# Masking the scores on GpSimd for two heads at once, and zero products in the values' PSUM banks

## The chip, the cores and the metric

The kernel runs on one NeuronCore of a Trainium2 chip. The metric is the device time of one execution in microseconds (us). Engines are named as the profile names them: PE is TensorE (its weight loads are PEld), DVE is VectorE, ACT is ScalarE, POOL is GpSimd, and SP is the engine that issues the DMAs.

## The reference: what is computed

Causal attention with a forgetting bias for 8 batches of 8 heads (576 positions, 64 columns a head, float32), and then a feed-forward block with a convolution of three taps and a gate.

```python
scores = scale * np.matmul(q, k.transpose(0, 1, 3, 2))
causal = np.triu(np.ones((S, S), dtype=bool), k=1)
cum = np.cumsum(np.maximum(s, 0.0), axis=-1)
bias = -(cum[:, :, :, None] - cum[:, :, None, :])
scores = np.where(causal, -1000000000.0, scores + np.minimum(bias, 0.0))
attn = np.exp(scores - np.max(scores, axis=-1, keepdims=True))
attn = attn / (np.sum(attn, axis=-1, keepdims=True) + 1e-09)
x = np.matmul(attn, v)                    # heads side by side: 8 x 576 x 512
...
h = np.maximum(x @ w_in, 0.0)             # 512 -> 1024
conv_out[t] = sum(conv_w[k] * h[t + k - 1] for k in range(3))
out = (h * (1.0 / (1.0 + np.exp(-conv_out)))) @ w_out      # 1024 -> 512
```

## The kernel before

**Work and its order.** Heads are worked on in 32 pairs: the two heads of a pair lie in the lower and the upper 64 partitions, and a product of 64 rows belongs to one of them. Four pairs make a batch, and when a batch's four pairs are done its feed-forward block follows. All work is written as tasks (`add(name, [(engine, planned duration)], dependencies, tag, ...)`). A list scheduler (`Sched.play`) then lays the tasks out once, when the program is built: at each moment it gives every engine the ready task with the smallest tag, where the planned durations say when an engine is free again. The tags come from the table `DUE`, one number for each task. What comes out is a fixed order of instructions for each engine. On the chip each engine works through its order strictly, and an instruction that waits holds up all that stand behind it.

**A pair.** The tasks of pair p, and the lines of the kernel before:

- The loads: `raw` (q and k), `bb` (the bias, spread over 128 partitions), `v`, `ek` (bias rows).
- `hi` and `lo` (L1032, L1036) split q and k into a rounded part and a rest. `lo` runs on POOL or DVE and takes all of `raw`.
- `sh0` to `sh3` (L1102): a first set of score products, in four parts with two PSUM banks each, of which only the row maxima are wanted. The causal mask is added by a product of a mask with a unit matrix (L1109) for the first seven pairs, and by a cut of `bb` on POOL (L1075) from then on. DVE takes the maxima (L1135).
- `turn` (L1161) transposes the maxima on PE. ACT copies them (L1169), and a DMA puts them into `eq`.
- `sc0` to `sc3` (L1209): the score products proper, four for each piece, the last of which (`eq`, `ek`) adds bias and maximum. For the first eight pairs (`p < B0`) a mask product on PE (L1213) stands in each of the five pieces with a diagonal, one for each head. For the other 24 pairs POOL zeroes the part above the diagonal after the exponential, ten `affine_select` a pair (L1244).
- The exponentials (L1231, ACT) go to the tiles `pt`, one for each head.
- From pair 7 on (`dense`) the exponentials of the key tiles 1 to 3 are added up, head by head, on DVE or POOL (L1292). `sum` (L1328, PE) makes the row sums, `pv` (L1269, PE) the product with the values into the two PSUM banks `pv`.
- The normalisation: ACT copies the sums (`gd`, L1344), DMAs gather them (`rc`), DVE takes the reciprocal (L1355), DMAs write it out and spread it (`ri_d`, `rb`), DVE multiplies (`nm`, L1378), ACT or DVE rounds (`xh`, L1393), DVE or POOL takes the rest (`xl`, L1397). `pv` of the next pair waits for `nm`.

The feed-forward products are L1428 (first) and L1517 (second); ACT, DVE and POOL do ReLU, taps, gate and splitting between them. From pair 8 on the products of a pair's attention stand together as one burst.

**Zero products.** Until the planned time `AWAKE` = 112 us the scheduler puts a product of zeros (L1564, `still`, 256 columns, result unused) into every planned gap of PE, one for each 0.12 us. It needs a free score bank (`ps`, six of them): with all six taken, PE gets none. If the last product worked on one head (mode "r"), the zero product has 64 rows; otherwise 128.

Of the kernel before, what the change touches and what calls it, by code (L numbers as in the profile page):

```python
# [65 lines left out]
B0 = 8  # L66
# [492 lines left out]
def kernel(  # L559
# [133 lines left out]
    def c_tt(n):  # L693
        return 0.155 + n / 0.96e3
# [134 lines left out]
    def rest(e):  # L829
        nc.vector.scalar_tensor_tensor(  # L830
            s_sb, cum, 8.0 * EK, grid, op0=ALU.subtract, op1=ALU.subtract
        )

    t_rest = add("rest", [("DVE", 1.5, True)], [t_cum], -140, rest)

    def bias_mm(e):
        for t in range(NT):
# [795 lines left out]
```

## Time and profile before

| what | value |
| --- | --- |
| time, median of 3 runs | 771.92 us (771.81 to 774.02) |
| profiled execution, its own time | 774.2 us |
| its span, first to last instruction | 772.5 us |
| PE busy / weight loads | 752.9 us (97%) / 669.8 us (87%) |
| DVE, ACT, POOL busy | 490.7 us (64%), 464.5 us (60%), 387.3 us (50%) |
| mean granted TensorE clock | 0.985 |
| zero products (L1564) | 149 |
| mask products in the scores (L1213) | 80 |
| `affine_select` on the exponentials (L1244) | 240 |
| additions of the exponentials (L1292) | 86 on DVE, 64 on POOL |

Read the table with the granted clock in mind: a busy PE counts zero products, mask products and slow products alike. All times below are from the span's start.

### The profile page before, as it was taken

How to read it: one execution, taken by the hardware profiler on the slowest of the kernel's cores; microseconds unless marked ns; L12 is line 12 of the kernel's file. 1: busy time of each engine (PE TensorE's matmuls, PEld its weight loads, DVE VectorE, ACT ScalarE, POOL GpSimd, SP SyncE). 2: the span in 40 equal slices, each digit the busy share in tenths (PEclk: the TensorE clock that was granted, in tenths of full speed). 3: DMA queues.
4: the chain of work that ended last, by engine and by line, in shares of the span. 5: the costliest groups of instructions: out<-in, count | busy, mean ns of one | idle time of the engine just before them, and what ended most of it. 6: DMA issues, size and time to landing. Idle time of an engine off the chain costs nothing.

```text
span 772.5 us, 20600 instructions
## 1 busy us (share of the span) xinstructions
PE 752.9 (97%) x7856; PEld 669.8 (87%) x7856; DVE 490.7 (64%) x1414; ACT 464.5 (60%) x1084; POOL 387.3 (50%) x575
## 2 busy tenths in 40 slices
PE   5999999999999999999999999999999999999998
PEld 4676678898888989898999989999999989999998
DVE  7478888456775756767564756756686756733622
ACT  5177678456566657657565757657565656644633
POOL 6032235355636566664735666646756565532211
PEclk8599999999999999999999999999999999999999
DMA  6857762332404242241423342232423230111000
GB/s 191 257 150 242 213 205 67 113 104 84 143 27 122 87 131 95 75 143 61 131 62 114 96 131 89 85 110 76 144 65 116 93 100 25 42 33 48 17 31 31
DMA packets 55160, 80.18 MB, mean 104 GB/s; under 512 B 14041, under 2 KB 34841, under 8 KB 55001
## 3 DMA queue, kind: packets, MB, share of 16 engines
q1 hardware_dynamic: 55061, 78.87, 33.1%
q8 instruction: 61, 1.00, 0.5%
q14 instruction: 38, 0.31, 0.1%
HBM read 67.48 MB, written 10.98 MB: 102 GB/s over the span
## 4 chain that ended last, share of the span: by engine, by line
PE 83%; DVE 6%; DMA 5%; issue 3%; ACT 1%; POOL 1%; SPq 0%; DVEq 0%; POOLq 0%; ACTq 0%
PE ps L1428 26%; PE ps L1517 26%; PE ps L1209 12%; PE pv L1269 10%; PE ps L1102 4%; DMA rb<-ri_d 3%; PE ps L1328 3%; DMA ri_d<-ri 2%; DVE ps L1135 2%; PE ps L1564 1%; DMA bb<-cum_d 1%; DVE r L1135 1%; PE ps L1213 1%; DVE w L909 0%; PE ps L1161 0%
## 5 line engine op out<-in xcount | busy, mean ns | idle before, releaser
L1428 PE MATMUL ps<-x,wi 128*128 128x290 f32 x1536 | 216.9, 298 | 1.6 <-DVE ct L1477 1.5
L1517 PE MATMUL ps<-u,wo 128*128 128x288 f32 x1536 | 217.0, 297 | 0.7 <-ACT ob L1534 0.5
L1428 PEld LDWEIGHTS ps<-x,wi 128*128 128x128 f32 x1536 | 209.1, 190 | 3.4 <-DVE ct L1477 1.8
L1517 PEld LDWEIGHTS ps<-u,wo 128*128 128x128 f32 x1536 | 206.5, 189 | 3.5 <-ACT ob L1534 0.7
L1231 ACT ACTIVATE pt<-ps,bias_sb 128x288 f32<-128x288 f32 (+4 forms) x384 | 153.6, 479 | 85.2 <-PE ps L1209 85.1
L1135 DVE CUSTOM_DVE_ANT_0 ps<-ps,bb 128x64 f32<-128x64 f32 (+4 forms) x320 | 132.2, 453 | 89.4 <-PE ps L1102 44.6
L1489 POOL TENSOR_TENSOR u<-ct,u 128x576 fp32r<-128x576 f32 x64 | 91.7, 1432 | 176.5 <-ACT u L1485 126.5
L1459 DVE SCALAR_TENSOR_TENSOR ct<-ps,cw_sb,ct 128x288 f32<-128x288 f32 (+1 forms) x256 | 130.8, 514 | 62.3 <-ACT ct L1446 59.4
L1209 PE MATMUL ps<-s 64*128 64x288 f32 (+4 forms) x1152 | 121.3, 305 | 4.7 <-DVE r L1135 3.5
L1209 PEld LDWEIGHTS ps<-s 64*128 64x128 f32 x1152 | 97.7, 186 | 15.3 <-DVE r L1135 9.4
L1036 POOL TENSOR_TENSOR s<-raw,s 128x1152 fp32r<-128x1152 f32 x31 | 83.7, 2698 | 51.8 <-DVE s L1032 30.2
L1269 PE MATMUL pv<-pt,v 128*32 128x448 f32 (+4 forms) x1536 | 94.7, 389 | 1.0 <-DVE rb L1378 0.9
L1075 POOL TENSOR_SCALAR_AFFINE_SELECT bb<-bb 128x256 f32<-128x256 f32 (+1 forms) x125 | 51.5, 421 | 79.7 <-DVE r L1135 41.5
L1441 ACT ACTIVATE ps<-ps 128x289 f32<-128x289 f32 x128 | 50.9, 397 | 62.5 <-PE ps L1428 61.4
L1269 PEld LDWEIGHTS pv<-pt,v 128*32 128x32 f32 x1536 | 59.4, 110 | 31.7 <-issue 24.5
L1244 POOL TENSOR_SCALAR_AFFINE_SELECT pt<-pt 128x128 f32<-128x128 f32 (+1 forms) x240 | 71.4, 321 | 13.8 <-ACT pt L1231 13.0
L1477 DVE TENSOR_TENSOR ct<-ct,ps 128x288 f32<-128x288 f32 x128 | 57.5, 449 | 29.9 <-ACT ct L1471 29.4
L1471 ACT ACTIVATE ct<-ct 128x288 f32<-128x288 f32 x128 | 56.3, 440 | 29.7 <-DVE ct L1459 29.2
L1209 PE MATMUL ps<-eq,ek 64*128 64x288 f32 (+4 forms) x384 | 69.1, 317 | 0.0
L1446 ACT ACTIVATE ct<-ps,cw_sb 128x288 f32<-128x288 f32 x128 | 63.6, 497 | 4.6
L1102 PE MATMUL ps<-s 64*128 64x288 f32 (+4 forms) x384 | 62.7, 347 | 0.0
L1135 DVE CUSTOM_DVE_ANT_0 ps<-ps,bb,r 128x288 f32<-128x288 f32 x64 | 30.9, 523 | 40.5 <-PE ps L1102 40.3
(89 smaller groups left out, 747.3 us busy)
## 6 DMA issues: line engine op xcount, KB each, us to landing
raw<-qk SPq DMA_DIRECT2D x32, 576.0 KB
bb<-cum_d SPq DMA_DIRECT2D x32, 576.0 KB
v<-vp SPq DMA_DIRECT2D x32, 320.0 KB
rb<-ri_d SPq DMA_DIRECT2D x64, 144.0 KB
outT<-ob SPq DMA_DIRECT2D x64, 144.0 KB
w<-w_in SPq DMA_DIRECT2D x8, 512.0 KB
w<-w_out SPq DMA_DIRECT2D x8, 512.0 KB
rows_d<-bx SPq DMA_DIRECT2D x1, 1215.0 KB
```

The source lines that it names most:

```text
L1036: tt_on(e)(st[:, 0:2, :], R_t[raw.slot], st[:, 2:4, :].bitcast(F32), op=ALU.subtract)
L1102: nc.tensor.matmul(dst[j], l, S_t[sb.slot][r, 2, c0:c1], start=True, stop=not (early and diagonal(tau, c1)),)
L1135: nc.vector.tensor_tensor_reduce(out=src, in0=src, in1=in1, scale=1.0, scalar=acc if c0 else -3.0e38, op0=ALU.add, op1=ALU.max, accum_out=acc,
L1209: nc.tensor.matmul(dst[j], l, m, start=(k == 0), stop=(k == 3))
L1231: nc.scalar.activation(PT_t[pts[j].slot][0:jt, O_T[t] + c0 : O_T[t] + c1], bank(pb, o, o + c1 - c0)[0:jt], AF.Sigmoid, bias=bias_sb[0:jt, ...
L1244: nc.gpsimd.affine_select(out=reg, in_=reg, pattern=[[1, dg]], compare_op=ALU.is_ge, fill=0.0, base=0, channel_multiplier=-1,)
L1269: nc.tensor.matmul(pvt[gs, o0 : o0 + c1 - c0], vt[0:jt, t, gs], PT_t[pts[g // 2].slot][0:jt, O_T[t] + c0 : O_T[t] + c1], start=(t == 0), s ...
L1428: nc.tensor.matmul(bank(hb, 0, XW), l, r, start=(k == 0), stop=(k == len(seq) - 1))
L1446: nc.scalar.activation(C_t[ct.slot][:, i, :], bank(hb, 2 * hf, 2 * hf + HS), AF.Copy, scale=cw_sb[:, 3 * f + 1 : 3 * f + 2],)
L1459: nc.vector.scalar_tensor_tensor(cc[:, lo:hi], bank(hb, hf + sh + lo, hf + sh + hi), cw_sb[:, 3 * f + k : 3 * f + k + 1], cc[:, lo:hi], op ...
L1489: tt_on(e)(uu[:, 1], C_t[ct.slot], uu[:, 0].bitcast(F32), op=ALU.subtract)
L1517: nc.tensor.matmul(bank(pb, 0, HS), l, r, start=(fp == 0 and k == 0), stop=(fp == NF // 2 - 1 and k == len(seq) - 1),)
```

## The change

1. **Zero products.** With no score bank free, a planned gap of PE now gets a zero product that writes to the values' banks `pv`, if these are free.
2. **Masks.** The mask products L1213 are gone. All 32 pairs are masked on POOL after the exponentials, and one `affine_select` does a piece for both heads: five a pair, twice as wide. It waits for the exponentials of both heads.
3. **Sums.** One addition does a key tile for both heads: three a pair from pair 7 on in the place of six, twice as wide. For that the tiles `pt` and `ht` become slices of one tile each.
4. **Plan.** Planned durations are changed (`SH_D`, `SC_D`, masks, sums and others), and the table `DUE` has new numbers, so the order on every engine is another one.

The table is shown by two lines, from its beginning.

```diff
-    -4342, -2961, -2916, -3027, -3033, -2954, -3077, -2973, -2965, -2830, -4716, -3541, -3351,
+    -4437, -31564, -3194, -3762, -3297, -3396, -3426, -2970, -2895, -2949, -3684, -32749, -26067,
...
-                    if now < idle[0] and free and now >= awake:
-                        slot = min(free, key=lambda i: idle[5].given[i])
+                    if now < idle[0] and (free or idle[6].free) and now >= awake:
+                        slot = min(free, key=lambda i: idle[5].given[i]) if free else -1
                         t = Task()
                         if mode != "r":
                             mode = None
                         t.name, t.mode, t.then = "idle", mode, []
                         lane = [0]
-                        lanes[slot].append(lane)
+                        if free:
+                            lanes[slot].append(lane)
                         t.emit = lambda e, slot=slot, mode=mode, lane=lane: idle[4](
...
-    PT_t = [const.tile([P, O_T[-1] + W_T[-1]], F32, name=f"pt{i}") for i in range(NPT)]
+    PT_a = const.tile([P, NPT, O_T[-1] + W_T[-1]], F32, name="pt")
+    PT_t = [PT_a[:, i, :] for i in range(NPT)]
...
-    H_t = [const.tile([P, 2, XW], F32, name=f"ht{i}") for i in range(NHT)]
+    H_a = const.tile([P, NHT, 2 * XW], F32, name="ht")
+    H_t = [H_a[:, i, :].rearrange("p (a c) -> p a c", a=2) for i in range(NHT)]
...
+    SH_D = 0.2, 0.2, 0.32, 0.33
+    SC_D = 0.54, 0.63, 1.18, 1.02
...
+        def both(r0, r1, c0, c1):
+            i0, i1 = (b.slot for b in pts)
+            return PT_a[r0:r1, i0 : i1 + 1 : i1 - i0, c0:c1]
...
-                        if k == 2 and c0 == 0 and p < B0:
-                            dg = min(P, cn)
-                            for j in range(2):
-                                nc.tensor.matmul(
-                                    dst[j][:, 0:dg], mask[:, MW - P : MW], unit[:, 0:dg],
-                                    start=False, stop=False,
-                                )
...
-            t_sc = add(f"sc{p}.{i}", [("PE", 4 * sum(c_rt(c1 - c0) for _, c0, c1 in part) + (0 if p >= B0 else 0.4))], [t_ident, t_shift, t_lo], A + 0.1 * i,
+            t_sc = add(f"sc{p}.{i}", [("PE", SC_D[i])], [t_ident, t_shift, t_lo], A + 0.1 * i,
...
-                    def sc_mask(e, j=j, t=t):
-                        jt, dg = J_T[t], min(P, W_T[t])
-                        reg = PT_t[pts[j].slot][0:jt, O_T[t] : O_T[t] + dg]
-                        nc.gpsimd.affine_select(
-                            out=reg, in_=reg, pattern=[[1, dg]], compare_op=ALU.is_ge, fill=0.0,
-                            base=0, channel_multiplier=-1,
-                        )
-
-                    if c0 == 0 and p >= B0:
-                        t_exp = add(f"mk{p}.{j}.{t}", [("POOL", 0.29, True)], [t_exp],
-                                    A + 0.1 * i, sc_mask, uses=[pts[j]])
                     masks.append((t, j, t_exp))
                     o += w
+            for t, c0, c1 in part:
+                if c0:
+                    continue
+
+                def sc_mask(e, t=t):
+                    reg = both(0, J_T[t], O_T[t], O_T[t] + min(P, W_T[t]))
+                    nc.gpsimd.affine_select(
+                        out=reg, in_=reg, pattern=[[0, 2], [1, min(P, W_T[t])]],
+                        compare_op=ALU.is_ge, fill=0.0, base=0, channel_multiplier=-1,
+                    )
+
+                done = [k for k, m in enumerate(masks) if m[0] == t]
+                t_mk = add(f"mk{p}.{t}", [("POOL", 0.42 if W_T[t] >= P else 0.3, True)],
+                           [masks[k][2] for k in done], A + 0.1 * i, sc_mask, uses=pts)
+                for k in done:
+                    masks[k] = (t, masks[k][1], t_mk)
...
-        def key_sum(j, t):
+        def key_sum(t):
             def run(e):
-                a = partial(j)
-                src = PT_t[pts[j].slot]
+                i0, i1 = (b.slot for b in acc)
+                a = H_a[:, i0 : i1 + 1 : i1 - i0, 0 : S - P]
                 o = P * (t - 1)
                 (nc.vector if e == "DVE" else nc.gpsimd).tensor_tensor(
-                    a[:, o:], src[:, P : S] if t == 1 else a[:, o:],
-                    src[:, O_T[t] : O_T[t] + W_T[t]], op=ALU.add,
+                    a[:, :, o:], both(0, P, P, S) if t == 1 else a[:, :, o:],
+                    both(0, P, O_T[t], O_T[t] + W_T[t]), op=ALU.add,
                 )
             return run
...
-                for j in range(2):
-                    t_ad = add(
-                        f"ad{p}.{j}.{t}",
-                        [("DVE", c_tt(W_T[t]), True), ("POOL", c_pool(W_T[t]), True, 2.0)],
-                        [m for k, h, m in masks if h == j and (k == t or t == 1 and k == 0)]
-                        + ([added[-2]] if t > 1 else []),
-                        tq - 4, key_sum(j, t), alloc=[acc[j]] if t == 1 else [],
-                        uses=[pts[j]] + ([acc[j]] if t > 1 else []),
-                    )
-                    added.append(t_ad)
+                t_ad = add(
+                    f"ad{p}.{t}",
+                    [("DVE", c_tt(2 * W_T[t]) + 0.07, True), ("POOL", c_pool(2 * W_T[t]), True, 2.0)],
+                    [m for k, h, m in masks if k == t or t == 1 and k == 0] + added[-1:],
+                    tq - 4, key_sum(t), alloc=acc if t == 1 else [],
+                    uses=pts + (acc if t > 1 else []),
+                )
+                added.append(t_ad)
...
-            ps_t[slot][:, 0:AWAKE_N], still[r, 0:P], still[r], start=True, stop=True
+            (pvt if slot < 0 else ps_t[slot])[:, 0:AWAKE_N], still[r, 0:P], still[r], start=True, stop=True
...
-        (AWAKE, t_still, 0.005 + AWAKE_N * 0.42e-3, AWAKE_T, stay_awake, pool_ps)
+        (AWAKE, t_still, 0.005 + AWAKE_N * 0.42e-3, AWAKE_T, stay_awake, pool_ps, pools["pv"])
```

Three places show how the order moves. The first is PE, after the maxima products of pair 0 have filled all six score banks (`ps_65` to `ps_70`); what follows are five transposes of the bias table (L838 before, L830 now) that need a bank given back. Before:

```order
L1102 MATMUL ps_69<-s_83 128x64
L1102 MATMUL ps_70<-s_83 128x64
L1109 LDWEIGHTS unit
L1109 MATMUL ps_69<-mask,unit 128x64
L1109 LDWEIGHTS unit
L1109 MATMUL ps_70<-mask,unit 128x64
L838 MATMUL ps_65<-ident,pt_97 128x64 x4
L838 MATMUL ps_65<-ident,pt_97 64x64
```

Now, the first two rows of the zero products that stand in between:

```order
L1104 LDWEIGHTS unit
L1104 MATMUL ps_69<-mask,unit 128x64
L1104 LDWEIGHTS unit
L1104 MATMUL ps_70<-mask,unit 128x64
L1559 LDWEIGHTS still
L1559 MATMUL pv<-still 128x256
```

and the last ones:

```order
L1559 LDWEIGHTS still
L1559 MATMUL pv<-still 128x256
L1559 LDWEIGHTS still
L1559 MATMUL pv<-still 128x256
L830 MATMUL ps_65<-ident,pt 128x64 x4
L830 MATMUL ps_65<-ident,pt 64x64
```

In all 56 zero products, which write to `pv`, now stand ahead of the transposes; they have 64 rows. Further on, 45 zero products stood between the transposes and pair 0's first score product; now there are 33. In the whole program there are 241 in the place of 149, all ahead of the first feed-forward product in both.

The second place is ACT, when pair 1's sums are ready and pair 0's normalised values are to be rounded. Before (`x<-rb` is pair 0's rounding, `rs<-ps` pair 1's copy of the sums, `rt` the next pair's maxima):

```order
L894 ACTIVATE w_5121_302<-w_10240_301 128x512
L899 ACTIVATE w_5122_303<-w_10240_301,tail_sb 128x512
L1393 CAST x<-rb 128x2x290
L1344 ACTIVATE rs<-ps_69 128x144
L894 ACTIVATE w_5121_308<-w_10240_307 128x512
L899 ACTIVATE w_5122_309<-w_10240_307,tail_sb 128x512
L1169 ACTIVATE rt_103<-ps_65,base_sb 10x64 x2
```

Now:

```order
L886 ACTIVATE w_5121_358<-w_10240_357 128x512
L891 ACTIVATE w_5122_359<-w_10240_357,tail_sb 128x512
L938 CAST wi<-w_5122_356 128x4x128
L1339 ACTIVATE rs<-ps_66 128x144
L1388 CAST x<-rb 128x2x290
L1163 ACTIVATE rt_101<-ps_65,base_sb 10x64 x2
```

The copy of the sums now stands ahead of the rounding, which waits for the normalisation of the pair before; it is so for the next pairs too.

The third place is POOL, after the last of its preparations (`v`), during the first pairs. Before:

```order
L717 AFFINE_SELECT v_95<-v_95 64x640
L1036 TENSOR_TENSOR s_83<-raw_81,s_83 128x1152
L949 TENSOR_TENSOR wi<-w_5122_306,wi 128x4x128
L1036 TENSOR_TENSOR s_84<-raw_82,s_84 128x1152
L1397 TENSOR_TENSOR x<-rb,x 128x2x290
```

Now:

```order
L709 AFFINE_SELECT v_95<-v_95 64x640
L1241 AFFINE_SELECT pt<-pt 128x2x128
L1241 AFFINE_SELECT pt<-pt 64x2x64
L1241 AFFINE_SELECT pt<-pt 128x2x128
L1031 TENSOR_TENSOR s_83<-raw_82,s_83 128x1152
L1241 AFFINE_SELECT pt<-pt 128x2x128 x2
L941 TENSOR_TENSOR wi<-w_5122_353,wi 128x4x128
L1241 AFFINE_SELECT pt<-pt 128x2x128 x2
L1031 TENSOR_TENSOR s_84<-raw_81,s_84 128x1152
```

The masks of the pairs' scores (`pt<-pt`) are new here, and the splitting of a later pair's q and k (`s<-raw,s`) stands between the masks of one pair.

## Rows read from the trace of the kernel before

**Rows 1.** Windows: us, busy per engine (instructions), granted clock, DMA share, GB/s

```profile
12.00:17.20 5.20, 0.00 (x0) 0.00 (x0) 2.48 (x7) 4.06 (x7) 3.79 (x5) 0.51 0.96 258
17.20:35.50 18.30, 18.27 (x90) 11.36 (x90) 10.25 (x47) 2.07 (x7) 0.00 (x0) 0.50 0.87 268
...
40.00:109.30 69.30, 67.39 (x935) 46.28 (x931) 56.24 (x161) 51.42 (x111) 19.70 (x11) 1.00 0.71 214
109.30:769.30 660.00, 654.03 (x6741) 602.63 (x6732) 411.29 (x1185) 398.08 (x946) 354.40 (x535) 1.00 0.28 85
```

**Rows 2.** PE, 0 to 50 us: start, length, line, operation, rows x columns, count

```profile
1.72 7.03 PE L1564 MATMUL ps<-still 128*128 128x256 bf16 x47 [1.72 <-DVE still L755]
...
17.23 0.80 PE L838 MATMUL ps<-ident,pt 64*128 64x64 f32 x5 [6.78 <-DVE r L1135]
...
27.42 4.87 PE L1564 MATMUL ps<-still 64*128 64x256 bf16 x22
...
34.34 1.09 PE L1209 MATMUL ps<-s 64*128 64x288 f32 x6
...
40.70 0.83 PE L1564 MATMUL ps<-still 64*128 64x256 bf16 x6
...
44.57 1.77 PE L1328 MATMUL ps<-pt,onehot 128*32 128x144 f32 x54
```

**Rows 3.** DVE, maxima of pairs 0 and 1; in brackets idle time and releaser

```profile
19.87 0.50 DVE L1135 CUSTOM_DVE_ANT_0 ps<-ps,bb 128x320 f32<-128x320 f32 x1 [0.24 <-PE ps L1109]
...
25.10 0.63 DVE L1135 CUSTOM_DVE_ANT_0 ps<-ps,bb 128x448 f32<-128x448 f32 x1 [1.39 <-PE ps L1109]
...
27.53 0.50 DVE L1135 CUSTOM_DVE_ANT_0 ps<-ps,bb 128x320 f32<-128x320 f32 x1 [0.50 <-PE ps L1109]
...
29.17 0.52 DVE L1135 CUSTOM_DVE_ANT_0 ps<-ps,bb,r 128x288 f32<-128x288 f32 x1
```

**Rows 4.** PE, 57 to 110 us, the first pairs

```profile
58.97 1.83 PE L1328 MATMUL ps<-pt,onehot 128*32 128x144 f32 x56
...
63.84 0.67 PE L1209 MATMUL ps<-s 64*128 64x288 f32 x6
...
64.89 0.56 PE L1209 MATMUL ps<-s 64*128 64x288 f32 x6
...
65.83 0.88 PE L1209 MATMUL ps<-s 64*128 64x448 f32 x6 [0.24 <-ACT pt L1231]
...
73.70 1.83 PE L1328 MATMUL ps<-pt,onehot 128*32 128x144 f32 x56
...
102.53 1.82 PE L1328 MATMUL ps<-pt,onehot 128*32 128x144 f32 x56
...
109.34 0.94 PE L1428 MATMUL ps<-x,wi 128*128 128x290 f32 x5
```

**Rows 5.** Chain of waits, 73 to 92 us: start, length, what

```profile
75.72 0.68 ACT x L1393
76.40 0.19 ACT rs L1344
...
80.37 3.37 DMA ri_d<-ri
...
84.35 6.01 DMA rb<-ri_d
...
90.48 0.06 DVE rb L1378
```

**Rows 6.** Groups by line on POOL: count, busy us, mean ns, idle before

```profile
L1036 POOL TENSOR_TENSOR s<-raw,s 128x1152 fp32r<-128x1152 f32 x31 | 83.7, 2698 | 51.8 <-DVE s L1032 30.2 <-issue 19.7 <-ACT s L1032 1.9
...
L1075 POOL TENSOR_SCALAR_AFFINE_SELECT bb<-bb 128x256 f32<-128x256 f32 x100 | 43.7, 437 | 79.7 <-DVE r L1135 41.5 <-DVE ri L1355 32.6 <-DMA rb<-ri_d 3.1
```

**Rows 7.** Windows of the mask products L1213 alone

```profile
109.30:773.00 663.70, 4.12 (x30) 1.70 (x30) 1.00 0.28 85
```

**Rows 8.** Additions of the exponentials, ns least/median/most

```profile
L1292 DVE TENSOR_TENSOR ht<-ht,pt x62: 344/492/4509, 164.2 to 688.0; 128x320 f32<-128x320 f32 x43, 128x192 f32<-128x192 f32 x19
```

More of the change, by code (lines that the diff above doesn't have):

```diff
@@ L832, in rest @@
         )
-    t_rest = add("rest", [("DVE", 1.5, True)], [t_cum], -140, rest)
+    t_rest = add("rest", [("DVE", 1.6, True)], [t_cum], -140, rest)
     def bias_mm(e):
@@ L1115, in pair @@
             w = sum(c1 - c0 for _, c0, c1 in part)
-            t_mm = add(f"sh{p}.{i}", [("PE", sum(c_rt(c1 - c0) for _, c0, c1 in part)
-                                           + 0.22 * early * sum(diagonal(tau, c1) for tau, _, c1 in part))],
+            t_mm = add(f"sh{p}.{i}", [("PE", SH_D[i] + 0.36 * early * sum(diagonal(tau, c1) for tau, _, c1 in part))],
                        [t_hi] + ([t_ident] if early else []),
@@ L1332, in sums @@
                     )
-        t_sum = add(f"sum{p}", [("PE", 0.62 if dense else 1.5)], [t_ident] + [m for _, _, m in masks] + added,
+        t_sum = add(f"sum{p}", [("PE", 0.63 if dense else 1.58)], [t_ident] + [m for _, _, m in masks] + added,
                     tq, sums, alloc=[sb_], uses=[*pts, *acc], mode="c32", burst=group(p + 1))
-        t_pv = add(f"pv{p}", [("PE", 2.82)], [t_v] + [m for _, _, m in masks], tq + 0.1,
+        t_pv = add(f"pv{p}", [("PE", 2.74)], [t_v] + [m for _, _, m in masks], tq + 0.1,
                    pv_mm(range(NT)), alloc=[pv], uses=[vb, *pts], mode="c32",
@@ L1350, in gather @@
                 nc.sync.dma_start(rc_t[j * D : (j + 1) * D], rs_t[j : 97 + j : 32])
-        t_rc = add(f"rc{p}", [("SP", 0.8)], [t_grd], tq, gather, uses=[ri], nbytes=4608)
+        t_rc = add(f"rc{p}", [("SP", 1.0)], [t_grd], tq, gather, uses=[ri], nbytes=4608)
         def inverse(e):
```

477 rows, old and new, of the table DUE are left out of this document.

## The prediction

> **What bounds the kernel now.** I read the busy times in windows first. From 109.3 us, where the first feed-forward product starts, to 769.3 us PE is busy for 654.0 of 660 us at a granted clock of 1.00, while DVE, ACT and POOL stay under two thirds [rows 1]. There only PE work that goes away, or new waits of PE, can move the end. Before 109.3 us PE looks busy too, but part of that is not work. The order of PE in time shows three losses. After the first batch of maxima products PE idles for 6.78 us, from 10.45 to 17.23 us, until DVE gives a bank back [rows 2]. The clock is at 0.51 from 12.0 us, and it stays at 0.50, the lower of the two levels (1.2 GHz), until after 35.5 us [rows 1]. In that stretch 22 zero products alone take 4.87 us, 0.22 us each, ahead of pair 0's first score product at 34.34 us; at full clock six take 0.83 us, of which the spacing is about 0.11 us [rows 2]. After that the pairs follow each other every 14 to 15 us: the sums start at 44.57, 58.97, 73.70 and, two pairs on, 102.53 us [rows 2, 4].
>
> The time to sum against is the profiled execution's, 774.2 us (span 772.5). The median of the three runs is 771.92 us, 2.3 us under it. I take the differences off the median. What a measurement of this kernel can tell from no change is about 0.3%, 2.3 us.
>
> **First score product.** If the 56 new zero products run at 0.11 us they fill 6.2 of the 6.78 us, and PE meets the bias transposes at 17.2 us as before, now at full clock. Then DVE sets the pace: its maxima of pairs 0 and 1 end at 29.7 us and lost 0.24, 1.39 and 0.50 us to PE [rows 3]. Without these they end at about 27.6 us. The transpose of pair 1's maxima (0.3 us) and five zero products (0.55 us) follow, so the first score product starts near 28.5 in the place of 34.34 us. The gain is 5.8 us. The trace has no row for zero products of 64 rows as the only work at full clock, so the gain has two ends: 5.8 us, and a loss worked out below as the first rival.
>
> **Mask products on PE.** In one cycle the piece of 288 columns with its two masks takes from 63.84 to 64.89, 1.05 us; the like piece without them takes from 64.89 to 65.83 less 0.24 us of wait, 0.70 us [rows 4]. So one diagonal piece costs 0.35 us. That is over the busy time alone: 30 products are 4.12 us after 109.3 us, 0.27 us a piece [rows 7]. I take 0.35 us, since it is start to start. Five pieces are 1.75 us a pair. Pairs 5 to 7 (30 of the 80 products, 15 pieces) lie behind 109.3 us where PE is the bound, so 5.2 us go there (4.1 us by the lower price).
>
> **Up to the first sums.** From the first score product to the first sums it was 34.34 to 44.57, 10.2 us [rows 2]. Take off 1.75 us of masks and about 0.7 us of half clock at its start, and add four zero products (0.4 us): 8.2 us. On POOL a mask for two heads is 0.44 us (the cut of 128x256), and a splitting of 2.70 us now stands between pair 0's masks [rows 6]; the maxima products of a later pair cover most of that, and I add 0.5 us. The sums then start near 37.2 us, 7.4 us earlier.
>
> **The first pairs.** From 44.57 to 109.34 us there are four more cycles and the last `sum` and `pv`. By PE's own order they lose four times 1.75 us of masks and gain about 40 zero products (4.4 us), so PE alone would be about 2.6 us shorter. But the normalisation takes its own time: the copy of the sums at 76.40 us, `ri_d` from 80.37 for 3.37 us, `rb` from 84.35 for 6.01 us, the multiplication at 90.48 us [rows 5]; a cycle cannot be much shorter than that chain less the sums. The copy waited 0.68 us behind `xh` on ACT [rows 5], which the new order takes away. I count 1.6 us of gain (0 to 2.6). The first feed-forward product then starts near 100.3 us, 9.0 us earlier.
>
> **The rest.** In the steady part the order has the same bursts, with a few more turns between products of 64 and of 128 rows: 116 changes, where before without the mask products there were 107. A piece with masks costs 0.08 us over its busy time for two such turns, so nine cost 0.4 us. Masks and additions for two heads come to fewer, longer instructions on engines that are a third idle; I count them at nothing, since at least 60 feed-forward products stand between a pair's last scores and its sums, some 6 us at the window's mean of 654 us over 6741 products [rows 1], against exponentials, two masks and two additions of 0.4 to 1 us. If that cover fails it is the third rival. The 6.0 us of idle PE could also shrink or grow with the new table; I take none.
>
> Sum: 9.0 + 5.2 - 0.4 = 13.8 us. 774.2 becomes 760.4 us, and the median **758.1 us**.
>
> **A rule about the clock.** PE was busy for 18.27 of 18.30 us from 17.20 us on at a clock of 0.50 [rows 1]; the 47 zero products of 128 rows at the start lifted it, the 22 of 64 rows did not [rows 2]. The Trainium skill (TensorE: Matmul & The Clock Gate, section "What's actually happening") says that the array is throttled by default and that activity releases it. By that rule alone zero products of any shape would keep the clock up, and the sum above stands; the trace does not bear it out for raising the clock, and no row here shows it for holding it.
>
> **Rivals.**
>
> First, *64 rows do not hold the clock*. It falls at 12.1 us or so as before. Then 15 of the 56 products run at 0.11 and 41 at 0.22 us, and the transposes start near 21.0 us, 3.8 us late. Twelve fewer zero products before the scores give 2.6 us back, so the scores start 1.2 us late; masks and cycles still gain. Sums 0.2 us earlier, cycles 1.6, masks 5.2, less 0.4: 765 us. If it falls one step later, nearer 761 us. For it: the 18 us at 0.50 under zero products of 64 rows. Against it: one such series is all that the trace has, and it began at the lower level.
>
> Second, *the transfers take the head start back*. From 40 to 109.3 us the DMA engines were 0.71 busy at 214 GB/s, and DVE 56.2 of 69.3 us [rows 1]. If weights and `rb` need the same time from about 30 us on, the cycles grow to 15.5 us, and some 5 us of the 9.0 are lost: 763 us. Against it: `rb` takes 6 us because it shares with weights that are only wanted at the first feed-forward block.
>
> Third, *slower*: a pair's sums wait for masks and additions. An addition on DVE has taken 4.5 us where 0.49 is the median [rows 8], so some wait behind something on POOL, and they are now twice as wide. The Trainium skill (SBUF — State Buffer, section "Who interferes with whom") has the two engines hold a shared port exclusively for a whole instruction; rows 8 agrees in kind, and no row shows which instruction held it. With 24 pairs, 0.58 us of wait for each eats the gain; at 1 us it is 782 us. Against it: the 6 us of cover.
>
> Fourth, the early stage gains nothing that lasts and the new order loses the masks' 5 us again: 771 us, no change.
>
> **Chances.** My forecast 0.58, the first rival 0.17, the second 0.15, the third 0.06, the fourth 0.04. Its own range is 753 to 763 us: down by 2 us of cycles and 3 us of steady idle, up by the lower price of the masks, no gain in the cycles and 2 us of new idle. With the first two rivals, 751 to 766 us. Only the third rival and the tail of the fourth are slower: faster 0.88, same 0.05, slower 0.07.
>
> **What would show it.** The clock 1.00 without a break from 5 us on, and the bias transposes near 17.2 us; first scores near 28.5 us, first sums near 37 us, first feed-forward product near 100 us; behind it a stretch shorter by 5 us with PE idle for about 6 us. A clock of 0.50 behind 15 us shows the first rival, cycles over 15 us the second. PE waits of over 10 us behind 110 us at the sums make me wrong.

## The result, and the profile after

The changed kernel takes 763.66 us (median of 4 runs, 761.29 to 766.71), against 772.56 us before (4 runs): ratio 0.9877, 95% interval 0.9853 to 0.9901. It is 1.2% faster; 1.8% was forecast. Its runs order themselves by the mean granted clock: 766.7 us at 0.989, 764.2 at 0.991, 763.1 at 0.996 and 761.3 us at 1.000. The profiled execution is the first of these (span 765.0 us).

Windows of the changed kernel, with columns as in [rows 1]:

```profile
10.50:17.60 7.10, 5.39 (x51) 4.41 (x48) 4.25 (x13) 5.86 (x9) 5.45 (x7) 1.00 0.73 219
17.60:20.00 2.40, 2.39 (x12) 1.49 (x12) 2.40 (x15) 0.73 (x2) 0.00 (x0) 0.53 1.24 347
20.00:32.50 12.50, 12.50 (x60) 7.14 (x59) 7.19 (x34) 1.00 (x4) 0.00 (x0) 0.50 0.90 279
...
34.90:41.70 6.80, 6.80 (x70) 5.09 (x68) 4.00 (x16) 6.45 (x15) 4.47 (x6) 1.00 0.27 83
...
105.48:765.00 659.52, 645.08 (x6708) 597.43 (x6702) 432.37 (x1165) 390.32 (x933) 320.15 (x379) 1.00 0.28 86
```

PE in time, answering [rows 2, 4]:

```profile
9.59 6.28 PE L1559 MATMUL pv<-still 64*128 64x256 bf16 x56
...
17.59 0.70 PE L830 MATMUL ps<-ident,pt 64*128 64x64 f32 x5 [1.71 <-DVE r L1129]
...
32.55 1.09 PE L1208 MATMUL ps<-s 64*128 64x288 f32 x6
...
54.90 1.83 PE L1323 MATMUL ps<-pt,onehot 128*32 128x144 f32 x56
...
105.48 1.21 PE L1423 MATMUL ps<-x,wi 128*128 128x290 f32 x7
```

The 56 zero products take 0.11 us each, and the clock is 1.00 under them and up to 17.6 us. Then PE idles for 1.71 us, because the series began early and ended early, and from about 18 us the clock is 0.50. It is 1.00 again from 34.9 us. The first score product starts 1.8 us earlier than before, the first sums start at 41.73 us (2.8 earlier), the first feed-forward product at 105.48 (3.9 earlier). From there to the end it is 659.5 us in the place of 663.2.

In the first pairs' cycles the copy of the sums is no longer behind the rounding, but it gains nothing. ACT in the second cycle:

```profile
56.17 0.69 ACT L886 ACTIVATE w<-w 128x512 f32<-128x512 f32 x1 [1.25 <-DMA w<-w_in]
56.75 0.74 ACT L891 ACTIVATE w<-w,tail_sb 128x512 uint32<-128x512 uint8 x1
57.40 0.60 ACT L938 CAST wi<-w 128x512 fp32r<-128x512 f32 x1
57.91 0.28 ACT L1339 ACTIVATE rs<-ps 128x144 f32<-128x144 f32 x1
```

and the chain of waits that goes on from it (answering [rows 5]):

```profile
59.90 0.54 DVE w L895
...
62.93 0.12 DVE ri L1350
...
63.41 4.51 DMA ri_d<-ri
...
68.55 4.32 DMA rb<-ri_d
...
73.32 0.77 DVE rb L1373
```

The copy starts 3.0 us behind the start of its sums (2.3 in the same cycle before; in the third cycle, that of [rows 5], it is 3.2 for 2.6), now behind the splitting of a weight piece that landed late. The reciprocal then stands behind more such work on DVE until 62.9 us, and the 4.5 KB of `ri_d` take 4.5 us. Weights are in the way on ACT and on DVE; what they do to the transfers is tested below (e11).

PE's waits behind 101 us (us in all, times, longest):

```profile
PE ps L1208 <- DVE r L1129: 7.5, 19, 0.5
PE ps L1097 <- DVE ct L1472: 1.1, 1, 1.1
PE ps L1208 <- DVE ct L1472: 0.8, 1, 0.8
```

Before, behind 110 us:

```profile
PE ps L1209 <- DVE r L1135: 3.1, 8, 0.4
PE ps L1428 <- DVE ct L1477: 1.5, 1, 1.5
```

With the shorter ones PE's idle time from the first feed-forward product to the end of the span went from 9.1 to 14.4 us, so the new order has more waits, above all of the score products for banks that DVE's maxima give back. DVE's additions behind the first of a pair (answering [rows 8]) have a median of 815 ns, and now and then far more:

```profile
L1289 DVE TENSOR_TENSOR ht<-ht,pt x37: 545/815/3647, 179.4 to 680.8; 128x640 f32<-128x640 f32 x19, 128x384 f32<-128x384 f32 x18
```

### The profile page after: what moved, and what is told of

It reads as the page before. It is cut to its first block, busy times and chain, and to the rows that moved or that the text cites. A ratio compares the mean times of both kernels' runs of the same rounds, so it can differ in the third digit from the quotient of the medians.

```text
span 765.0 us, 20449 instructions
## 1 busy us (share of the span) xinstructions
PE 744.2 (97%) x7868; PEld 669.3 (87%) x7868; DVE 513.5 (67%) x1404; ACT 455.6 (60%) x1070; POOL 363.1 (47%) x444
## 4 chain that ended last, share of the span: by engine, by line
PE 79%; DVE 8%; issue 5%; DMA 4%; ACT 2%; POOL 1%; SPq 0%; DVEq 0%; POOLq 0%; ACTq 0%
PE ps L1423 25%; PE ps L1512 25%; PE ps L1208 11%; PE pv L1266 10%; PE ps L1097 4%; DVE ps L1129 3%; PE ps L1323 3%; DMA rb<-ri_d 2%; DMA ri_d<-ri 2%; ACT pt L1223 1%; PE ps L1559 1%; DVE r L1129 1%; DMA bb<-cum_d 1%; DVE ct L1454 1%; DVE rb L1373 1%
## 5 line engine op out<-in xcount | busy, mean ns | idle before, releaser
L1223 ACT ACTIVATE pt<-ps,bias_sb 128x288 f32<-128x288 f32 (+4 forms) x384 | 152.9, 479 | 64.6 <-PE ps L1208 64.4
L1129 DVE CUSTOM_DVE_ANT_0 ps<-ps,bb 128x64 f32<-128x64 f32 (+4 forms) x320 | 134.3, 451 | 47.3 <-PE ps L1097 23.1
L1208 PE MATMUL ps<-s 64*128 64x288 f32 (+4 forms) x1152 | 113.8, 304 | 8.6 <-DVE r L1129 7.5
L1208 PEld LDWEIGHTS ps<-s 64*128 64x128 f32 x1152 | 91.0, 187 | 17.3 <-DVE r L1129 12.4
L1241 POOL TENSOR_SCALAR_AFFINE_SELECT pt<-pt 128x256 f32<-128x256 f32 (+1 forms) x160 | 69.9, 450 | 74.6 <-ACT pt L1223 56.4
L1031 POOL TENSOR_TENSOR s<-raw,s 128x1152 fp32r<-128x1152 f32 x31 | 88.8, 2865 | 6.2 <-ACT s L1027 3.9
L1472 DVE TENSOR_TENSOR ct<-ct,ps 128x288 f32<-128x288 f32 x128 | 57.1, 449 | 21.7 <-ACT ct L1466 20.9
L1097 PE MATMUL ps<-s 64*128 64x288 f32 (+4 forms) x384 | 60.3, 348 | 1.3 <-DVE ct L1472 1.1
L1208 PE MATMUL ps<-eq,ek 64*128 64x288 f32 (+4 forms) x384 | 59.7, 301 | 0.0
L1129 DVE DVE_READ_ACCUMULATOR2_ANT r<- 128x1 f32 x384 | 54.1, 141 | 0.0
```

What stands on the lines that cost most here:

```text
L1031: tt_on(e)(st[:, 0:2, :], R_t[raw.slot], st[:, 2:4, :].bitcast(F32), op=ALU.subtract)
L1097: nc.tensor.matmul(dst[j], l, S_t[sb.slot][r, 2, c0:c1], start=True, stop=not (early and diagonal(tau, c1)),)
L1129: nc.vector.tensor_tensor_reduce(out=src, in0=src, in1=in1, scale=1.0, scalar=acc if c0 else -3.0e38, op0=ALU.add, op1=ALU.max, accum_out=acc,
L1208: nc.tensor.matmul(dst[j], l, m, start=(k == 0), stop=(k == 3))
L1223: nc.scalar.activation(PT_t[pts[j].slot][0:jt, O_T[t] + c0 : O_T[t] + c1], bank(pb, o, o + c1 - c0)[0:jt], AF.Sigmoid, bias=bias_sb[0:jt, ...
L1241: nc.gpsimd.affine_select(out=reg, in_=reg, pattern=[[0, 2], [1, min(P, W_T[t])]], compare_op=ALU.is_ge, fill=0.0, base=0, channel_multipl ...
```

## The experiments

All derive from the changed kernel unless they say otherwise; the edits change what a task emits and leave the planned order alone. Each was timed against the kernel before on the same chip.

**The clock.** Four kernels ask what the zero products bring and why the clock falls.

First, a longer series (e1):

```diff
+            bridged[0] += 1
+            again = bridged[0] <= 56 and bridged[0] % 4 == 0
+        for _ in range(1 + again):
             nc.tensor.matmul(
```

> Edit: 14 more zero products among the 56 that write to the values' banks, so that they last to about 17.4 us and PE does not idle for 1.71 us ahead of the bias transposes. Gap theory (the 64-row zero products hold the clock, and it is the idle piece behind them that lets it fall, in some executions and not in others): the clock is at 1.00 from 5 us on without a break, the first score product starts at 28.5 to 30 us, all runs lie close together at 760 to 761 us, level with the fastest run of the changed kernel (761.3) and 3 us below its median (763.7). Shape theory (64-row products do not keep the clock up for long, or the weak stretch is the one behind the transposes): it falls near 18 us all the same, with a first score product near 32.5 us and 763 to 767 us.

Measured: 764.42 us (761.09 to 770.2), ratio 0.9895 (0.9861 to 0.9929), so no gain. PE of its profiled execution, and then its windows:

```profile
9.82 7.81 PE L1566 MATMUL pv<-still 64*128 64x256 bf16 x70
17.54 0.51 PE L830 MATMUL ps<-ident,pt 64*128 64x64 f32 x5
18.25 0.37 PE L1097 MATMUL ps<-s 64*128 64x288 f32 x1 [0.20 <-ACT eq L744]
18.80 0.39 PE L1097 MATMUL ps<-s 64*128 64x288 f32 x1 [0.18 <-DVE r L1129]
```

```profile
18.00:19.00 1.00, 0.62 (x3) 0.36 (x2) 1.00 (x7) 0.19 (x1) 0.00 (x0) 1.00 1.52 401
...
20.00:25.00 5.00, 5.00 (x31) 2.84 (x30) 4.90 (x24) 0.50 (x2) 0.00 (x0) 0.66 0.89 215
```

The 1.71 us are gone, 0.38 us of idle time behind them stay, and the clock falls 3.9 us later, at 21.6 us. The large gap was not the only cause.

Second, none of the zero products in the values' banks (e2):

```diff
     def stay_awake(slot, mode, lane):
+        if slot < 0:
+            return
```

> Edit: of the changed kernel, the zero products for which no score bank is free are left out (the rest of the program stands in the same order). If the zero products in the values' banks bring what they bring through the clock: it falls near 11 us as before the change, stays low until about 35 us, and the time is 765 to 768 us, 2 to 4 us over the changed kernel. If they bring nothing (the clock falls in the changed kernel too): 763 to 764 us, no difference.

Measured: 766.38 us (764.81 to 767.25), all runs at 0.984 to 0.987, ratio 0.9908 (0.9883 to 0.9932). So masks, sums and order bring some 7 us alone; the zero products bring 2 to 3 us on the median, and 5 where the clock holds.

Third, 128 rows (e3):

```diff
-        r = slice(D * lane, D * lane + D) if mode == "r" else slice(0, P)
+        r = slice(D * lane, D * lane + D) if mode == "r" and slot >= 0 else slice(0, P)
```

> Edit: of the changed kernel, the zero products in the values' banks work on 128 rows in the place of 64; their number stays 56, and so does the idle piece behind them. Gap theory: as the changed kernel, the clock falls behind the idle piece in some runs, 761 to 767 us, median near 763.7. Shape theory (128 rows leave the clock in a state that outlasts 1.7 us of idle time): no fall, 760 to 761 us in all runs.

Measured: 762.65 us (759.92 to 765.84), ratio 0.9863 (0.9832 to 0.9894). Four of five runs were at 1.00. In the profiled one of these the long series began 1.3 us later than in the changed kernel (10.90 us) and the bank came back 0.5 us sooner (17.11 us), there was no gap, and the first score product started at 26.44 us:

```profile
26.44 0.66 PE L1208 MATMUL ps<-s 64*128 64x288 f32 x6
...
101.35 0.94 PE L1423 MATMUL ps<-x,wi 128*128 128x290 f32 x5
```

Fourth, the zero products alone, in the kernel before (e4):

```diff
-                    if now < idle[0] and free and now >= awake:
-                        slot = min(free, key=lambda i: idle[5].given[i])
+                    if now < idle[0] and (free or idle[6].free) and now >= awake:
+                        slot = min(free, key=lambda i: idle[5].given[i]) if free else -1
```

> Edit: the kernel before with the zero products in the values' banks alone; masks, sums and the table are those of before, and the order is the same but for the zero products. Before ran at 772.6 us. If the part is worth what the changed kernel's records say (the clock falls 6 us later, and a first score product about 2 us earlier): 770 to 771 us. If the clock is held through: first scores near 28.5 us and 767 us. If all of the gain comes from masks and order: 772 to 773 us.

Measured: 774.05 us (768.55 to 776.27), ratio 1.0008 (0.9985 to 1.0030). At a clock of 0.998 and 1.000 it took 769.3 and 768.6 us, otherwise 771 to 776, as long as before: in the profiled execution the clock fell at 18 us and stayed low until about 38.5. There a fall 6 us later gained nothing: the rise came 2.5 us later too, and the first score product no sooner (34.71 for 34.34 us).

The rows were then tried in all zero products (e5, `r = slice(0, P)`):

> Edit: all zero products, those in the score banks too, work on 128 rows; their number and place stay. Four of five runs of the kernel with 128 rows in the values' banks alone had a mean clock of 1.00, against 3 of 22 runs with 64 rows (three kernels). Rows theory (128 rows keep the clock up behind the zero products, 64 rows do not): every run at a clock of 1.00, 760 to 763 us, median 761. Rival (the fall hangs on how the loads happen to land, and rows do nothing): several runs at 0.985 to 0.995 with 764 to 767 us. If the turns between 64-row score products and 128-row zero products cost PE more than the 0.1 us that a zero product has taken: 2 us more than 761.

Measured: 763.08 us (761.07 to 765.17), ratio 0.9877 (0.9849 to 0.9905), clocks of 0.993 to 1.000. The rows theory fell: over all kernels that leave some idle piece of PE open, a mean clock of 0.997 or more ("held" from here on) came in 5 of 22 runs with 64 rows (the changed kernel, e1, e4) and in 13 of 41 with 128 (e3, e5, and e6, e7, e8, e12 below). The 4 of 5 in e3 had misled me: e6, e8 and e12, which are e3 up to the first score product, held it in 4 of 24. A held clock can still have one short fall: the profiled execution of e5 (0.998) was at 0.50 from 98.7 to 102.1 us, behind a wait of 2.25 us.

Last, work at every place where PE had idled, with 64 rows (e9) and with 128 (e10); `fill` issues zero products to `pv`, and the long series is that of e1:

```diff
     def bias_mm(e):
+        bias_products(e)
+        fill(3)
...
                     o += c1 - c0
+                filled[0] += 1
+                if 4 <= filled[0] <= 8:
+                    fill(2)
```

> Edit: the changed kernel (64-row zero products) with 14 more zero products in the long series, three behind the bias transposes and two behind each of the next five parts of the maxima products, all to the values' banks, so that PE has work at each place where it idled between 14 and 20 us in the profiled executions whose clock fell (the changed kernel 1.71 us, the first experiment 0.38 us, and four more; in the two whose clock held, PE did not idle there). Gap theory: the clock is at 1.00 in all or nearly all runs, first scores at 26 to 29 us, median 760 to 762 us. Rows theory (64-row work lets it fall whatever the gaps): most runs at 0.985 to 0.995, 763 to 766 us. Cost theory (the additional products delay the maxima products by more than they give): clock at 1.00 and 763 us or more.

> Edit: the same additional zero products, with 128 rows for all that write to the values' banks. Gap theory: as the one with 64 rows, 760 to 762 us, all runs at 1.00. Rows theory: all runs at 1.00 here, 760 to 762 us, but not with 64 rows. If neither gaps nor rows decide: several runs at 0.985 to 0.995 in both.

Measured: e9 764.13 us (761.03 to 773.8; ratio 0.9902, 0.9872 to 0.9932), with 7 of 11 runs at 0.999 or more and these at 761.0 to 764.5; e10 764.64 us (760.89 to 766.87; 0.9898, 0.9870 to 0.9926), 5 of 6 at 0.997 or more. With e11 below 16 of 21 runs held the clock, against 18 of 63 with the gaps, so idle pieces are a cause of the fall. It isn't the chip that was used: e12, with the gaps, ran on that of e9 to e11, and none of its 8 runs held the clock. The traces agree. In the nine whose clock fell ahead of the first scores (both kernels, e1, e2, e4, e6, e7, e8, e12) PE has 0.3 to 7.8 us of idle time between 10 us and the fall; in the five that held it (e3, e5, e9, e10, e11) PE has no piece over 0.06 us there before 24.9 us. But idle pieces are not the whole of it. 4 of e9's runs lost the clock (0.982 to 0.991), and no trace of these was kept; and in e3 PE waited longer later on, at a clock of 1.00 before and after:

```profile
69.59 1.93 PE L1266 MATMUL pv<-pt,v 128*32 128x128 f32 x24 [2.81 <-DVE rb L1373]
```

Nor does a held clock make it 761 us each time: at 1.00 the runs still differ by 3 us.

**The masks.** Mask products back on PE for eight pairs (e6, on e3):

```diff
+                        if k == 2 and c0 == 0 and p < B0:
+                            dg = min(P, cn)
+                            for j in range(2):
+                                nc.tensor.matmul(dst[j][:, 0:dg], mask[:, MW - P : MW], unit[:, 0:dg], start=False, stop=False)
...
                 def sc_mask(e, t=t):
+                    if p < B0:
+                        return
```

> Edit: the kernel with 128 rows in the values' banks, but with the mask products on PE again for the first eight pairs, and POOL without a mask for these. Its profiled execution had the first sums at 35.6, the first feed-forward product at 101.4 and 659.6 us from there to the end. By the prediction's price (0.35 us a piece less the turns) the last stretch grows by 4.8 to 5.2 us; by the start-to-start times of the two traces (28.4 us of attention work of the first pairs behind the first feed-forward product before, 22.5 after) it grows by 5.9 us. Before it: if PE's own work paces the cycles, each of the four grows by 1.75 us and the first feed-forward product comes at 108 us; if the normalisation and its transfers pace them, the masks vanish in PE's waits and it comes at 102 to 104 us. In all 766 to 772 us. If POOL's masks were no cheaper for PE than the products: no difference, 762 us.

Measured: 779.12 us (775.05 to 779.37), ratio 1.0078 (1.0054 to 1.0103): slower than before. Its span is 775.7 us, and it has

```profile
110.18 1.08 PE L1432 MATMUL ps<-x,wi 128*128 128x290 f32 x6
```

so 665.5 us to the end, 6.0 more than e3. Against e1, whose clock did the same (0.991, span 763.8 us), first scores to first sums grew from 10.0 to 11.7 us, from there to the first feed-forward product from 62.9 to 67.5 us: 12 us in all, half of it behind the first feed-forward product.

**Pairing.** Masks and additions one head at a time, in the same places (e8, on e3):

```diff
-                    reg = both(0, J_T[t], O_T[t], O_T[t] + min(P, W_T[t]))
+                    for b in pts:
+                        reg = PT_t[b.slot][0 : J_T[t], O_T[t] : O_T[t] + min(P, W_T[t])]
...
+                for j in range(2):
+                    a = partial(j)
+                    src = PT_t[pts[j].slot]
```

> Edit: as the one with 128 rows in the values' banks, but each mask and each addition for two heads is issued as two instructions, one for each head, in the same place. If pairing is at nothing, as predicted: 659.6 us from the first feed-forward product to the end, within 0.5 us, with POOL and DVE busier by some 15 us each. If the wide instructions hold up the maxima and so cause the 7.5 us of PE's waits for score banks: 656 to 658 us, these waits near 3 us. If the pairing is itself a gain, since the split additions end later and the maxima behind them too: 661 us or more.

Measured: 768.61 us (766.41 to 776.97), ratio 0.9967 (0.9936 to 0.9998). The first feed-forward product is at 101.91 us of a span of 767.0, so 665.1 us behind it, 5.5 more. Its waits of PE:

```profile
PE ps L1208 <- DVE r L1129: 7.5, 19, 0.5
PE ps L1425 <- DVE ct L1474: 1.3, 2, 0.8
...
PE ps L1425 <- DVE x L1394: 1.0, 3, 0.4
```

The 19 waits for score banks are the same to a tenth, so the wide instructions don't cause them. Pairing, which I had counted at nothing, is worth 5.5 us in this order, which was planned for it. Without it the stretch is 2 us longer than in the kernel before (663.2), although that still has the mask products. About half of the 5.5 us shows as waits of feed-forward products for taps and splittings and of sums for additions; the other half is spread over them.

**The transfers.** Half of the weights' bytes (e7 on e3, e11 on e10):

```diff
+                elif split > 1:
+                    nc.sync.dma_start(dst[:, 0 : split // 2], s32[:, 0 : split // 2])
+                else:
+                    nc.sync.dma_start(dst[:, :, 0:n], s32[:, :, 0:n])
```

> Edit: as the one with 128 rows in the values' banks, but each of the 16 weight pieces loads half of its bytes and uses them twice, so the feed-forward products work on other weights; all else stands in the same order. Transfers theory (the second rival: the cycles of 13 to 17 us are set by transfers that share the queues with the weights): the four cycles together fall from 59.7 us to 56 us or less and the first feed-forward product comes at 97 us or sooner. Chain theory (the steps of the normalisation take that long by themselves): 59 to 60 us, the first feed-forward product at 101 us, and the same time within 1 us.

Measured: 765.89 us (759.51 to 769.05), ratio 0.9917 (0.9883 to 0.9951). The clock fell in the profiled execution (0.988), the four cycles took 57.1 us (58.0 in e1, where they start late too) and the first feed-forward product came at 105.1, so this could not decide what happens to an early start. With the clock held it could:

> Edit: as the one before with 128 rows, and each of the 16 weight pieces loads half of its bytes and uses them twice (the feed-forward products work on other weights). It asks what takes a head start back: from the first sums to the first feed-forward product it was 65.7 and 67.6 us in the two profiled executions that reached the first sums at 35.6 us, and 62.9 to 63.8 us where these came at 41 us. Transfers theory (the weights land no sooner, so an earlier start only waits longer): with half the weights it is 62 us or less, the first feed-forward product comes 3 us sooner than in the kernel with whole weights, and the time is 757 to 759 us where that is at 760 to 762. Chain theory: no difference.

Measured: 759.42 us (758.26 to 760.86), ratio 0.9836 (0.9812 to 0.9860), all four runs at 1.00. Its first feed-forward product:

```profile
97.62 1.08 PE L1454 MATMUL ps<-x,wi 128*128 128x290 f32 x6
```

PE's wait for the normalisation before it (us, times, longest), in e10 and then in e11:

```profile
PE pv L1281 <- DVE rb L1388: 5.5, 4, 2.4
```

```profile
PE pv L1297 <- DVE rb L1404: 0.2, 1, 0.2
```

From the first sums to the first feed-forward product it is 60.9 us, against 64.6 and 66.0 us in e9 and e10. The transfers theory holds: where the start is early, the weights take 4 to 5 us back between these two points. The first feed-forward product comes 2.5 us sooner than in e9 and 5.9 us sooner than in e10 (e11's own sums start at 36.8 us, theirs at 35.5 and 37.5). From the reciprocal to the multiplication, where the two transfers of the normalisation stand, it is 8.3 to 9.3 us in the four cycles of e11 against 9.3 to 11.2 in e9 and e10, so this piece, almost all of it transfers, is shorter with fewer bytes of weights beside it.

**Additions that stand still.** In the changed kernel seven of DVE's additions took over 1.9 us, each while POOL worked on a splitting. Each ends a fixed time behind the end of an instruction of POOL: 0.41 to 0.42 us for the three of 128x384 elements, 0.68 to 0.69 for the three of 128x640, 0.95 for the one of 128x896. They were sent to POOL (e12, on e3):

```diff
+                if e == "DVE":
+                    on_dve[0] += 1
+                    if on_dve[0] - 1 in (12, 17, 23, 32, 36, 40, 47):
+                        e = "POOL"
```

> Edit: the kernel with 128 rows in the values' banks, in which the seven additions that took DVE over 1.9 us (3.65 us where 1.24 is usual, each while POOL worked on a splitting of its own; two such before the change) are issued on POOL in the same place of the program. Port theory (DVE's addition stands still while POOL's splitting runs, and the taps behind it come late): PE's wait of 1.15 us at 485 us goes away, and the stretch from the first feed-forward product to the end is 658.5 us or less in the place of 659.6. Rival (DVE is late for its own work, and POOL's additions then hold up sums or splittings): the wait stays or moves to the sums, 659.5 us or more. The time can hardly show it: 760 to 763 us where the clock holds.

The expectation's 1.24 us are a mean with the slow ones in it; the median is 1.00 us. Measured: 767.17 us (765.53 to 768.78), ratio 0.9927 (0.9902 to 0.9952), clocks of 0.986 to 0.993; 660.2 us from the first feed-forward product (103.79 us) to the end of the span (764.0). Both waits for `ct` (1.1 and 0.8 us) are gone. But a later addition now stands in the place of the one moved. DVE, POOL and PE around it, in this order, then the window behind:

```profile
489.91 3.41 DVE L1295 TENSOR_TENSOR ht<-ht,pt 128x384 f32<-128x384 f32 x1
...
488.25 2.69 POOL L1033 TENSOR_TENSOR s<-raw,s 128x1152 fp32r<-128x1152 f32 x1
490.91 1.39 POOL L1490 TENSOR_TENSOR u<-ct,u 128x576 fp32r<-128x576 f32 x1
492.27 0.64 POOL L1072 TENSOR_SCALAR_AFFINE_SELECT bb<-bb 128x256 f32<-128x256 f32 x2
...
493.38 0.44 PE L1329 MATMUL ps<-ht,onehot 128*32 128x144 f32 x4 [1.68 <-DVE ht L1295]
```

```profile
494.00:496.00 2.00, 2.00 (x30) 1.17 (x27) 0.79 (x3) 0.29 (x1) 0.00 (x0) 0.51 0.40 148
```

The addition, 0.56 us in the median of the changed kernel, ends 0.41 us after the last of these instructions of POOL, which follow each other without a break. Its `sum` waits 1.68 us, and the clock falls for 3.4 us, which makes 46 of the `pv` products take 4.55 us where they take 2.87. The port theory's mechanism stands, its gain does not: what the move gave elsewhere (1.7 us in the feed-forward products, 1.0 us in the one burst of attention that had taken 9.8 us) this one burst took back, 12.6 us for 9.3. The wait moved to the sums.

## Why the prediction came out as it did

The forecast was 758.1 us, the time is 763.7. That is in the range of 751 to 766 us, which counts the first two rivals, and 0.7 us outside the forecast's own of 753 to 763. A part of each of these two rivals came true, and the last stretch came out near its forecast in part by luck. The steps, with the profiled execution, and with the profiled ones that held the clock (e3, e5, e9, e10):

| step | forecast | profiled | clock held |
| --- | --- | --- | --- |
| first score product, us | 28.5 | 32.55 | 26.4 to 27.9 |
| first sums, us | 37.2 | 41.73 | 35.5 to 37.5 |
| from there to the first feed-forward product | 63.1 | 63.75 | 64.6 to 67.6 |
| first feed-forward product, us | 100.3 | 105.48 | 100.1 to 103.6 |
| from there to the end | 658.4 | 659.5 | 659.6 to 659.7 |

(The 67.6 us are e5's, with its 3.4 us at 0.50 in them.)

**First score product.** The step that failed is "PE meets the bias transposes at 17.2 us as before, now at full clock". It took the 6.2 us of zero products as lying in a gap of 6.78 that stays put. They began 0.9 us earlier (9.59 for 10.45), DVE gave the bank back 0.4 us later, 1.71 us stayed open, and the clock fell; by e1, filling that gap alone moves the fall and doesn't prevent it. Where the clock holds, the first scores come at 26.4 to 27.9 us, even sooner than forecast. The first rival ("64 rows do not hold the clock") is wrong as stated: they hold it, for as long as they last, and rows make no difference that the runs show (e5). The row that spoke for it, 22 zero products of 64 rows at 0.50, had ten of 128 rows near it at 0.50 too (at 25.18 and 32.49 us in the kernel before).

**Masks.** The mechanism was right, the price a little low. Behind the first feed-forward product I had 5.2 us less 0.4 for turns; e6 gives 6.0. In e6 they also cost the first pairs 1.7 us, and the cycles 4.6.

**Cycles.** I forecast 1.6 us of gain from the sums to the first feed-forward product; it was 1.0, and where the head start is whole there is none (64.6 to 67.6 us, 64.8 before). "The copy waited 0.68 us behind `xh` on ACT, which the new order takes away" failed: weights took that place. The second rival is right in kind: e11 shows that it costs 4 to 5 us once the clock holds. In the profiled execution it costs less, for the start came later (e7 and e1, both late: 57.1 and 58.0 us for the four cycles).

**The rest.** The prediction put two terms at nothing, pairing ("I count them at nothing") and a change of PE's idle time under the new table ("I take none"). Both failed, and against each other: pairing gives 5.5 us (e8), and PE is idle for 5.3 us more. Counting start to start over the PE records, the first pairs' attention work behind the first feed-forward product went from 28.4 to 22.5 us (masks), the 23 full bursts of the later pairs, 132 products each, from 198.9 to 201.5, and the feed-forward products lost 0.3: together the 3.7 us measured. Of the 2.6 us added some 1.6 are in two bursts in which DVE came late (9.7 and 9.3 us, where the median is 8.7); the other 1.0 is spread. Pairing isn't its cause (e8), so by exclusion it is the new order, which was not tested alone; by e8 and e6 it would cost some 8 us without pairing (665.1 us against 663.2 less 6.0), an estimate. That the two nearly cancel is luck. The third rival's mechanism is there, seven additions held up in the place of two, but by e12 it costs PE some 2.7 us, of which 1.9 us are the waits for `ct`, and not 0.58 us a pair: the cover of feed-forward products is mostly deep enough.

What stays open is why the clock, with no gap left ahead of the first scores in the profiled execution, still fell in 4 of e9's 11 runs, which loads that land at other times could do, and why these took 769 to 774 us, more than other kernels at such a clock. No variant is clearly faster than the changed kernel with all its weights: e3 and e5 lie within its interval.

## What to carry to other kernels

Filling an idle stretch with work sized to the stretch of one trace leaves a gap as soon as the work ahead of it moves; the filler has to last until the instruction that ends the wait in every run. A head start is worth only what the next resource grants: ask, before adding it to the sum, whether the loads that are needed at its end come any sooner. An instruction that is "hidden" and twice as wide needs its neighbours looked at, those that POOL runs at the same time too, and not only its own cover. And two terms that are put at nothing can be large and cancel: test each alone.

## What the runs showed of the hardware

- The clock's level decides 5 us here, and the same program keeps or loses it from run to run (761.3 us at 1.000, 766.7 at 0.989). The Trainium skill (TensorE: Matmul & The Clock Gate, section "What's actually happening") says that the chip judges activity on a time base of its own, which doesn't start with the kernel; the spread agrees in kind, and no run here separates it from loads that land at other times.
- Once down, the clock stayed at 0.50 under 12.5 us of fully busy PE in the changed kernel (20.0 to 32.5 us: 36 products of 64 rows, 24 of them zero products, and 22 of 128 rows, 8 of them zero products). In the nine traces with a fall ahead of the first score products it rose 1.5 to 4.1 us after these (32.55 and 34.8 us in the changed kernel, 34.71 and 38.5 in e4). What in this work raises it, no run tells apart.
- PE's waits of 1.68 us amid the steady work (e12) and of 2.25 us at 96.5 us (e5) were each followed by 3.4 us at 0.50; one of 2.81 us at 66.8 us (e3) was not.
- An addition with both inputs in SBUF on DVE took 3.41 us where 0.56 is the median, and ended 0.41 us behind the last of POOL's instructions that ran meanwhile. The Trainium skill (SBUF — State Buffer, section "Who interferes with whom") says that a DVE instruction with two SBUF inputs contends with a GpSimd instruction that reads SBUF; e12 agrees.
